# q and k loaded once per batch, their pooled sums taken from PSUM, and layer one's float64 words landing in place

## The chip, the core and the metric

One NeuronCore of a Trainium2 chip runs the whole kernel in one launch. The metric is the device time of that launch in microseconds (us). Three runs of the kernel before took 962.6, 950.5 and 953.72 us, so its median is 953.72. The traces come from a profiled execution, which took 953.08 us.

In the rows, PE is TensorE's matmul stream and PEld its weight loads, DVE is VectorE, ACT is ScalarE, POOL is GpSimd, and SP is SyncE, whose queue issues all the DMAs spoken of here. PSUM is the memory that TensorE writes and that DVE and ACT read.

## The reference

Inputs are q, k, v of [4 batches, 8 heads, 576 tokens, 64] in float32 and two pairs of float64 weights, w_in [512, 2048] and w_out [2048, 512]. The attention has two branches, and their sum goes through two layers:

```
q_d, k_d, v_d = mean of every 4 tokens of q, k, v          # 144 pooled tokens
out_up    = repeat(softmax(q_d k_d^T / 8) v_d, 4 times)    # pooled attention
mask      = |i - j| < 4
out_local = softmax(where(mask, q k^T / 8, -1e9)) v        # band attention
x = (out_up + out_local) as [2304 tokens, 512]
x = relu(x @ w_in1)^2 @ w_out1                             # layer one
y = relu(x @ w_in2)^2 @ w_out2                             # layer two
```

## The kernel before

**Matmuls.** Every fp32 product of the two layers is made of three passes over a high and a low part of both factors (xH, xL and w..0, w..1). The 2304 tokens are 9 tiles of 256, and d_ff is cut into 8 slices p of 256 columns. A step is one slice for one tile: the first product h (L868), then relu and square on ACT and the split into high and low on ACT and DVE (helper `low_g`), then the second product y (L950; in layer two, seven products at L933). Layer one's steps 0 to 15 take tiles 0 and 1 in turns, slice by slice; step 16 is the first of tile 2, step 72 the first of layer two, and there are 144.

**Weights.** The weights arrive as 64-bit words. `convert` takes half of a (slice p, kind) pair, 128x512 words, into one of the landing buffers, and ACT (L698, L700, L373) and DVE (L702, L706, L719) turn them into a high and a low fp32 part. Layer two's pairs are converted too, and written to scratch in DRAM for a later reload. There are four landing buffers ld0 to ld3. Some weight buffers whose words come late serve as further landing buffers, or as buffers of the softmax, until then (the names e..).

**Attention.** Local attention works in groups of 116 queries, five to a batch. Before, `group` loads 128 tokens of q and of k for each (L547, in runs of 256 bytes), transposes them on PE (L556, 8 matmuls), and ACT copies the result out of PSUM (128x1024). Then come the mask (L574), the scores (L583), the softmax on DVE and ACT (L594 to L616), its transposes (L620), and the product with v (L638; v in `values`, 64-KB loads at L532), which with `outd` of the pooled branch gives xr (L650). `split_x` makes xH and xL (L846).

The pooled branch loads q and k a second time in `pool_qk`: six loads of 384 KB per batch (L419), whose runs are 3072 bytes long; two adds per load (L423, L425), on DVE for batches 0 and 1 and on POOL for 2 and 3; three transposes (L431); and two copies by ACT into qd or kd. `pool_v` does as much for v (L403, L407). `heads_of` then makes scores (L454), softmax (L459 to L474), transposes (L481) and the product with the pooled v (L492), and ACT copies it to outd.

**The order.** Each engine's instructions stand in one fixed sequence, written by a planner (class `Order`) from costs in `dve`, `act`, `pool`, `dma` and from due times: every job (a load, a conversion, a head, a group) is a thread in a lane, and constants such as CP, CD (conversions), GP (groups), QP (q and k) and HP (heads) say for which tile it is due. An engine can't pass an instruction that waits. `fill` puts small bf16 matmuls (L1105) into the gaps that the planner sees on PE ahead of the first layer product.

Of the kernel before, what the change touches and what calls it, by code (L numbers as in the profile page):

```python
# [8 lines left out]
F32 = mybir.dt.float32  # L9
# [11 lines left out]
GD = S // 4  # L21
# [14 lines left out]
NLD, NGA, NQK, NVW, NPB, NHD = 4, 2, 2, 2, 2, 2  # L36
AHEAD = 4
LEAD = 2
XO = 'PQVL'
XN = [2, 2, 2, 3]  # L40
# [6 lines left out]
CP, CD, GP, UP = -0.7, 0, -1.92, -0.78  # L47
QP, VP, HP = -0.52, 0.0, 0.05
# [159 lines left out]
def attention_two_mlp_kernel(  # L208
# [19 lines left out]
    mask16 = [sb.tile([128, 64], BF16, name=f"mask{i}") for i in range(3)]  # L228
    nmb_ = [sb.tile([128, 2, H], F32, name=f"nmb{i}") for i in range(NPB + 2 * XN[0])]
    nm_ = [sb.tile([72, 2, 4], F32, name=f"nm{i}") for i in range(NHD)]  # L230
# [4 lines left out]
    ODD = (0, 4)  # L235
    RISE, FALL, JOIN = {1: 0, 2: 48}, {1: 16, 2: 0}, 5
    wt = {}

    def weight(p, kind, low, layer=1):

        if kind == 0:
            if (p, low) not in wt:
                odd = 64 * (low and p in ODD)
                w = sb.tile([128, odd + 1024], F32R, name=f"w{p}0{low}", tag=f"w{p}0{low}")
                wt[p, low] = [w[:, odd + 256 * k - 4 * (odd > 0 and k == 0):][:, 0:256] for k in range(4)]
                wt[p, low, "all"] = w.rearrange("p (k f) -> p k f", k=4) if not odd else None
                if odd:
                    wt[p, low, 0] = w[:, odd - 4:odd + 516].rearrange("p (k f) -> p k f", k=2)[:, :, 0:256]
                else:
                    wt[p, low, 0] = w[:, 0:512].rearrange("p (k f) -> p k f", k=2)  # L250
                wt[p, low, 1] = w[:, odd + 512:odd + 1024].rearrange("p (k f) -> p k f", k=2)
            return wt[p, low]

        if p < JOIN:
            c = FALL[layer] + 2048 * p
            w = joint
        else:
            shift = FALL if p == 6 else RISE
            if p not in wt:
                wt[p] = sb.tile([128, 2048 + max(shift.values())], F32R, name=f"w{p}1", tag=f"w{p}1")  # L260
            c = shift[layer]
            w = wt[p]
        return w[:, c + 1024 * low:c + 1024 * low + 1024].rearrange("p (f e) -> p f e", f=2)

    gSL = sb.tile([128, 512], F32R, name="gSL")
    ga = [sb.tile([128, 512], F32, name=f"ga{i}", tag=f"ga{i}") for i in range(NGA)]
    early = {}
    for p in (7, 6):
        for low in (1, 0):
            early[p, 0, low] = sb.tile([128, 1024], F32, name=f"e{p}0{low}", tag=f"w{p}0{low}")  # L270
    for p in range(6):
        for low in range(2):
            weight(p, 0, low)
    for p in (7, 6, 5):
        w = sb.tile([128, 2048 + max((FALL if p == 6 else RISE).values())], F32, name=f"e{p}1", tag=f"w{p}1")
        for low in range(2):
            early[p, 1, low] = w[:, 1024 * low:1024 * low + 1024]
    joint = sb.tile([128, 2048 * JOIN + 16], F32R, name="w_out")
    g_ = sb.tile([128, 2048 + 48], F32R, name="g")

# [30 lines left out]
    f_at, f_xr, f_ld, f_ga = Slots(3), Slots(NXR), Slots(NLD, NLD), Slots(NGA)  # L311
    f_vw, f_qk, f_pb, f_hd = Slots(NVW, NVW), Slots(NQK, NQK), Slots(NPB, NPB), Slots(NHD)
# [62 lines left out]
    def dma(nbytes, run=4096):  # L375

        return "SP", nbytes / (16e3 * run / (8.0 + run * 0.037))
# [33 lines left out]
    def pool_qk(b, src, dst, c):  # L411

        if b == 1:
            yield o.at("h", 0, 1)
        n = yield from f_ld.take(b == 0)
# [6 lines left out]
        yield own(b, dve(384), pool(384))  # L422
# [3 lines left out]
        if b:  # L426
            yield o.at("scored", b - 1)
# [732 lines left out]
```

## Time and profile before

| | us |
|---|---|
| median of three runs | 953.72 |
| profiled execution | 953.08 |
| span of its trace | 951.30 |
| first layer product (step 0) | 66.18 |
| tile 2's first product (step 16) | 202.06 |
| layer two's first product (step 72) | 564.01 |

The span runs from the first to the last instruction; 1.8 us of the execution lie outside it. Mean granted clock of TensorE is 0.986 of full speed. Over the span PE is busy 95%, DVE 52%, ACT 58%, POOL 17%, and DMAs move 101.0 MB. These shares mix stages that differ, so the rows below are given by stage: the attention ahead of step 0, steps 0 to 15, the rest of layer one, layer two.

### The profile page before, as it was taken

What the parts mean: (1) busy time and instruction counts of PE and PEld (TensorE: products, weight loads), DVE (VectorE), ACT (ScalarE), POOL (GpSimd) and SP (SyncE); (2) the same over time, 40 slices, a digit from 0 to 9 for tenths busy, and PEclk for the clock granted to TensorE, in tenths of its full rate; (3) what the DMA queues carried; (4) which work ended last, traced back from release to release, by engine and by line L of the source; (5) the groups of instructions that cost most, each with busy time, mean ns of one, the idle gap of its engine ahead of it and who ended that gap; (6) DMA issues with size and microseconds to landing.
All of it is one profiled execution on the core that took longest, in us unless ns stands there. A gap on an engine that the chain in (4) does not pass through costs nothing.

```text
span 951.3 us, 21354 instructions
## 1 busy us (share of the span) xinstructions
PE 908.4 (95%) x8792; PEld 867.4 (91%) x8792; DVE 494.7 (52%) x1042; ACT 550.2 (58%) x1109; POOL 160.5 (17%) x158
## 2 busy tenths in 40 slices
PE   8786998989999999999999999999999999999996
PEld 4456997979999999999999999999999999999996
DVE  4789687234454565654321216555554555545464
ACT  3678796445656766665453657645454554545543
POOL 1000001016245200101354454201010110101000
PEclk9999999989999999999999999999999999999999
DMA  9877775127438557676131444011010101100000
GB/s 225 168 185 195 223 195 153 30 79 173 94 111 191 151 174 233 216 233 204 63 101 34 156 156 129 28 45 45 1 45 2 45 1 46 45 1 24 1 23 23
DMA packets 99553, 101.00 MB, mean 106 GB/s; under 512 B 66688, under 2 KB 72320, under 8 KB 99456
## 3 DMA queue, kind: packets, MB, share of 16 engines
q1 hardware_dynamic: 99456, 99.64, 36.9%
q8 instruction: 69, 1.13, 0.5%
q14 instruction: 28, 0.23, 0.1%
HBM read 80.74 MB, written 18.87 MB: 105 GB/s over the span
## 4 chain that ended last, share of the span: by engine, by line
PE 82%; DVE 4%; DMA 4%; ACT 4%; issue 1%; SPq 0%; ACTq 0%; DVEq 0%
PE h L868 37%; PE y L950 17%; PE at L933 13%; PE y L933 5%; DMA ld<-in_v_dram 2%; DMA ld<-in_moe_w_in_dram 1%; PE at L950 1%; PE at L556 1%; PE at L583 1%; PE at L492 1%; PE at L638 1%; PE h L1105 1%; PE at L481 1%; PE at L454 1%; PE at L620 1%
## 5 line engine op out<-in xcount | busy, mean ns | idle before, releaser
L868 PE MATMUL h<-xH,w 128*128 128x256 f32 x2304 | 315.1, 279 | 0.0
L868 PEld LDWEIGHTS h<-xH,w 128*128 128x128 f32 x2304 | 286.3, 189 | 1.4 <-issue 0.6
L879 ACT ACTIVATE h<-h 128x512 f32<-128x512 f32 x144 | 83.9, 583 | 173.8 <-PE h L868 169.3
L868 PE MATMUL h<-xL,w 128*128 128x256 f32 x1152 | 178.6, 277 | 0.0
L917 DVE TENSOR_TENSOR g<-h,g 128x512 fp32r<-128x512 f32 x144 | 98.6, 684 | 133.6 <-ACT g L890 133.5
L868 PEld LDWEIGHTS h<-xL,w 128*128 128x128 f32 x1152 | 152.9, 188 | 0.0
L913 DVE TENSOR_TENSOR S<-h,S 128x128 f32<-128x128 f32 x144 | 42.0, 292 | 160.5 <-ACT g L890 156.4
L950 PE MATMUL y<-g,w_out 128*128 128x256 f32 x960 | 122.0, 282 | 0.0
L950 PEld LDWEIGHTS y<-g,w_out 128*128 128x128 f32 x960 | 115.2, 191 | 0.9 <-issue 0.6
L846 POOL TENSOR_TENSOR xL<-xr,xH 128x512 fp32r<-128x512 f32 x30 | 39.5, 1333 | 353.7 <-ACT xH L373 353.7
L896 ACT CAST SH<-S 128x512 fp32r<-128x512 f32 x72 | 44.8, 622 | 90.7 <-DVE S L913 88.8
L881 ACT ACTIVATE h<-h 128x512 f32<-128x512 f32 x144 | 84.1, 584 | 3.4
L890 ACT CAST g<-h 128x512 fp32r<-128x512 f32 x144 | 84.5, 587 | 2.0 <-DVE S L913 0.7
L950 PE MATMUL y<-g,w 128*128 128x256 f32 x576 | 72.2, 280 | 0.0
L950 PEld LDWEIGHTS y<-g,w 128*128 128x128 f32 x576 | 67.9, 188 | 1.9 <-issue 1.2
L922 DVE TENSOR_TENSOR gSL<-S,SH 128x512 fp32r<-128x512 f32 x72 | 54.3, 754 | 10.2 <-ACT SH L896 1.2
L702 DVE SCALAR_TENSOR_TENSOR ld<-ld 128x512 int32<-128x512 int32 x64 | 44.4, 694 | 27.8 <-ACT ld L700 27.6
L698 ACT ACTIVATE ga<-ld 128x512 f32<-128x512 f32 x64 | 43.2, 674 | 21.3 <-DMA ld<-in_moe_w_in_dram 5.3
L706 DVE SCALAR_TENSOR_TENSOR ga<-ga,ld 128x512 int32<-128x512 int32 x64 | 45.6, 713 | 1.2
L423 POOL TENSOR_TENSOR ld<-ld 128x384 f32<-128x384 f32 x12 | 13.1, 1093 | 186.4 <-DVE hd L474 154.4
L913 DVE TENSOR_TENSOR S<-S,h 128x128 f32<-128x128 f32 x144 | 41.3, 287 | 5.3 <-ACT g L890 0.7
L700 ACT ACTIVATE ld<-ld 128x512 uint32<-128x512 uint32 x64 | 42.8, 668 | 0.1
(265 smaller groups left out, 1368.3 us busy)
## 6 DMA issues: line engine op xcount, KB each, us to landing
ld<-in_moe_w_out_dram SPq DMA_DIRECT2D x32, 512.0 KB, 4.0
ld<-ws SPq DMA_DIRECT2D x24, 512.0 KB, 3.3
ld<-in_moe_w_in_dram SPq DMA_DIRECT2D x32, 256.0 KB, 5.1
ld<-in_moe_w_in_dram SPq DMA_DIRECT2D x16, 512.0 KB, 3.9
ws<-ga SPq DMA_DIRECT2D x32, 256.0 KB, 3.0
ys<-ld SPq DMA_DIRECT2D x9, 512.0 KB, 2.8
xr<-ys SPq DMA_DIRECT2D x9, 512.0 KB, 4.8
vw<-in_v_dram SPq DMA_DIRECT2D x68, 64.0 KB, 2.9
```

Of the source, the lines that this page charges most:

```text
L702: nc.vector.scalar_tensor_tensor(out=w32[:, :, 0], in0=w32[:, :, 1], scalar=-2 ** 31, in1=w32[:, :, 0], op0=ALU.bitwise_and, op1=ALU.bitwi ...
L706: nc.vector.scalar_tensor_tensor(out=gi, in0=gi, scalar=3, in1=w32[:, :, 0], op0=ALU.logical_shift_left, op1=ALU.bitwise_or)
L868: nc.tensor.matmul(out=o, lhsT=w[kk][:, fs], rhs=x[:, kk], start=(i == 0), stop=(i == len(mms) - 1))
L879: nc.scalar.activation(out=h, in_=h, func=AF.Relu)
L881: nc.scalar.activation(out=h, in_=h, func=AF.Square)
L890: nc.scalar.copy(g_of(i, 0), h)
L896: nc.scalar.copy(late2["SH"], late2["S"])
L913: nc.vector.tensor_tensor(out=dst, in0=a, in1=b, op=op)
L917: nc.vector.tensor_tensor(out=g_of(i, 1), in0=h, in1=g_of(i, 0).bitcast(F32), op=ALU.subtract)
L922: nc.vector.tensor_tensor(out=gSL, in0=late2["S"], in1=late2["SH"].bitcast(F32), op=ALU.subtract)
L933: nc.tensor.matmul(out=seven(n, m - 1), lhsT=lhsT, rhs=quarter(p, w, low), start=p == 0 and x == 0 and m not in (2, 3, 6), stop=p == NP - ...
L950: nc.tensor.matmul(out=yb[e // 2][:, (e % 2) * 256:(e % 2) * 256 + 256], lhsT=w[:, fi, e * 128:e * 128 + 128], rhs=g[:, fi * 256:fi * 256 ...
```

## The change: what it does

- `load_qk` takes the place of `pool_qk` and of the loads in `group`. A batch's q and k come once, in five chunks of 128 tokens (the last has 64), in runs of 256 bytes. A chunk is transposed (L431, 8 matmuls), ACT copies it out to `qkT`, and DVE sums every 4 tokens of the same PSUM tile into `qkd` (L438, a `tensor_reduce` over 128x1024). There is one `qkT` for all batches, so a chunk of batch b waits for the local scores of batch b-1 that read it, and for that batch's pooled scores.
- `heads_of` waits for the pooled v and for all local groups of the batch before ahead of its transposes; there is one `outd` instead of two.
- `convert1` loads the words of a whole pair into the buffer that will hold the pair's parts, and converts 1024 wide, or in two halves of 512 (ga0, ga1). Layer two's conversion is `convert2`, as before in halves of 512.
- The landing buffers are ld0, ld1 and gp instead of four; gp is lent to the conversions of layer one until these are done. The buffers lent early change (XO, XN). Conversions are due 0.55 tiles apart (CD), heads 0.15 tiles earlier (HP), and the planner's price of a DMA rises.

```diff
-CP, CD, GP, UP = -0.7, 0, -1.92, -0.78
-QP, VP, HP = -0.52, 0.0, 0.05
+CP, CD, GP, UP = -1.2, 0.55, -2.0, -0.78
+QP, VP, HP = -0.52, 0.0, -0.1
...
-        return "SP", nbytes / (16e3 * run / (8.0 + run * 0.037))
+        return "SP", nbytes / (16e3 * run / (10.0 + run * 0.047))
...
-    def pool_qk(b, src, dst, c):
-
+    def load_qk(b, c):
+
+        n = min(128, S - 128 * c)
         if b == 1:
             yield o.at("h", 0, 1)
-        n = yield from f_ld.take(b == 0)
-        lf = ld[n].bitcast(F32)
-        t = lf[:, 0:768].rearrange("p (g r d) -> p g r d", g=3, r=4)
-        yield dma(128 * 3072, 3072)
-        nc.sync.dma_start(
-            out=lf[:, 0:768], in_=src[b].rearrange("h (p g) d -> (h p) (g d)", p=16)[:, c * 768:(c + 1) * 768]
+        i = yield from f_ld.take(b < 2)
+        raw = ld[i].bitcast(F32)[0:n].rearrange("p (z e) -> p z e", z=2)
+        for z in range(2):
+            tt = yield dma(n * 2048, 256)
+            nc.sync.dma_start(
+                out=raw[:, z].rearrange("p (h d) -> p h d", h=H),
+                in_=(q, k)[z][b, :, 128 * c:128 * c + n].rearrange("h s d -> s h d"),
+            )
+        if b:
+            for g in range(max(0, c - 1), min(NG, c + 2)):
+                yield o.at("lscored", b - 1, g)
+            yield o.at("scored", b - 1)
+        yield lambda: tt
+        a = yield from f_at.take()
+        yield "PE", 0.9
+        for z in range(2):
+            for m in range(4):
+                nc.tensor.transpose(pair[a][:, z, 128 * m:128 * m + n], raw[:, z, 128 * m:128 * m + 128], ident[0:n, 0:n])
+        got = pair[a].rearrange("p z (m s) -> p z m s", m=4)[:, :, :, 0:n]
+        tt = yield act(8 * n)
+        evac(qkT[:, :, :, 128 * c:128 * c + n], got)
+        f_ld.put(i, tt)
+        ev["qkT", b, c] = tt
+        tt = yield dve(8 * n)
+        nc.vector.tensor_reduce(
+            out=qkd[:, :, :, 32 * c:32 * c + n // 4], in_=got.rearrange("p z m (g r) -> p z m g r", r=4),
+            op=ALU.add, axis=AX.X,
         )
...
         yield own(b, dve(576), dve2(576), pool(576))
         engine().tensor_tensor(out=p4, in0=p4, in1=sm.unsqueeze(2).to_broadcast([72, 4, GD]), op=ALU.mult)
+        yield o.at("vpooled", b)
+        if b:
+            yield o.at("local", b - 1)
         a = yield from f_at.take()
...
+        st = early[p, kind] if (p, kind) in early else buffer(p, kind, I64, "s")
+        st = st[:, 0:1024]
...
+        m = yield from f_ga.take()
+        parts = [(gp, 0, 1024)] if m == 0 else [(gb[i], 512 * i, 512) for i in range(2)]
```

**The order at three places.** On SP, the start of the program before: six pooled loads of q and k come first, and the loads of the local groups after them.

```order
L419 DMA ld0_106<-in_q_dram 128x768
L419 DMA ld1_107<-in_k_dram 128x768
L419 DMA ld2_108<-in_q_dram 128x768
L419 DMA ld3_109<-in_k_dram 128x768
L419 DMA e601_81<-in_q_dram 128x768
L419 DMA e600_82<-in_k_dram 128x768
L547 DMA e51_97<-in_q_dram 128x8x64
L547 DMA e51_97<-in_k_dram 128x8x64
```

And now: ten loads of chunks, and then v and the first weights.

```order
L418 DMA ld1_104<-in_q_dram 128x8x64
L418 DMA ld1_104<-in_k_dram 128x8x64
L418 DMA e61_95<-in_q_dram 128x8x64
L418 DMA e61_95<-in_k_dram 128x8x64
L418 DMA e61_95<-in_q_dram 128x8x64
L418 DMA e61_95<-in_k_dram 128x8x64
L418 DMA e60_92<-in_q_dram 64x8x64
L418 DMA e60_92<-in_k_dram 64x8x64
L396 DMA e60_92<-in_v_dram 72x4x256
L396 DMA e51_96<-in_v_dram 72x4x256
L396 DMA ld0_103<-in_v_dram 72x4x256
L659 DMA s00_86<-in_moe_w_in_dram 64x2x256 x2
```

The pooled loads are gone, the local chunks stand in their place, and v and the weights follow.

On PE, the last instructions ahead of tile 2's first product (the last row), before. hd0 and hd1 are the pooled softmax of batch 1, at0 is the one PSUM tile that all of these use:

```order
L481 MATMUL at0_123<-ident_63,hd0_121 72x72 x8
L950 MATMUL at1_124<-g_99,w61_1623 128x256 x8
L950 MATMUL at1_124<-g_99,w71_1796 128x256 x16
L492 MATMUL at0_123<-hd0_121,vd_118 64x144 x4
L950 MATMUL at1_124<-g_99,w71_1796 128x256 x8
L481 MATMUL at0_123<-ident_63,hd1_122 72x72 x8
L492 MATMUL at0_123<-hd1_122,vd_118 64x144 x4
L638 MATMUL at0_123<-pb0_114,vw0_112 64x58 x16
L638 MATMUL at0_123<-pb1_115,vw1_113 64x58 x16
L574 LDWEIGHTS ident16_64
L574 MATMUL at0_123<-mask1_66,ident16_64 128x256
...
L556 MATMUL at0_123<-ident_63,ld3_109 128x128 x8
L868 MATMUL h0_126<-xH0_100,w000_83 128x256
```

And now, around the same product (the row of L858 with x8):

```order
L941 MATMUL at1_116<-g_94,w61_1509 128x256 x16
L431 MATMUL at0_115<-ident_63,ld1_104 128x128 x8
L941 MATMUL at1_116<-g_94,w61_1509 128x256 x8
L941 MATMUL at1_116<-g_94,w71_1716 128x256 x24
L604 MATMUL at0_115<-ident_63,pb0_83 128x128 x4
L858 MATMUL h0_118<-xH0_97,w00_457 128x256 x8
L858 MATMUL h0_118<-xL0_99,w00_457 128x256 x4
L622 MATMUL at0_115<-pb0_83,vw0_106 64x58 x16
```

Batch 1's heads now stand between steps 4 and 11 and the products with v of its first two groups at steps 13 and 14; one transposed chunk, one softmax transpose and the third group's product with v (L622) are left here.

On SP, the queue of the same stretch now. ys is the result of layer one on its way to DRAM, vw are the v rows of a local group:

```order
L418 DMA gp_105<-in_q_dram 128x8x64
L418 DMA gp_105<-in_k_dram 128x8x64
L418 DMA ld0_103<-in_q_dram 128x8x64
L418 DMA ld0_103<-in_k_dram 128x8x64
L537 DMA vw0_106<-in_v_dram 64x4x64 x4
L537 DMA vw1_107<-in_v_dram 64x4x64 x4
L1056 DMA ys0_120<-ld1_104 128x1024
L537 DMA vw0_106<-in_v_dram 64x4x64
L418 DMA ld1_104<-in_q_dram 64x8x64
L418 DMA ld1_104<-in_k_dram 64x8x64
L537 DMA vw0_106<-in_v_dram 64x4x64 x3
```

The third group's v (the last row) now stands behind a load into ld1, and that behind the store of ys0 from ld1.

## Rows read from the trace of the kernel before

**Rows 1.** Windows by stage: stretch, us; busy us (xinstructions) per engine; PEclk, DMA share, GB/s

```profile
0.00:24.00 24.00, 19.81 (x127) 10.44 (x128) 10.01 (x25) 7.51 (x15) 3.03 (x18) 1.00 0.93 224
24.00:66.20 42.20, 34.28 (x452) 21.77 (x450) 34.75 (x77) 29.53 (x73) 0.00 (x0) 0.93 0.76 170
66.20:101.50 35.30, 26.96 (x281) 25.31 (x280) 29.71 (x57) 29.00 (x51) 0.00 (x0) 0.89 0.82 208
101.50:154.60 53.10, 50.12 (x439) 48.94 (x438) 42.16 (x75) 45.41 (x90) 0.00 (x0) 1.00 0.74 202
154.60:202.10 47.50, 38.60 (x405) 35.44 (x403) 18.92 (x38) 20.24 (x52) 7.71 (x8) 0.91 0.19 53
202.10:564.00 361.90, 361.90 (x3838) 351.44 (x3837) 154.46 (x277) 215.80 (x434) 112.38 (x109) 1.00 0.51 150
564.00:951.30 387.30, 376.77 (x3266) 374.05 (x3264) 204.71 (x498) 202.70 (x396) 37.40 (x23) 1.00 0.10 35
```

**Rows 2.** Timeline of PE at two first products: start us, us, instruction xcount

```profile
66.18 1.66 PE L868 MATMUL h<-xH,w 128*128 128x256 f32 x8
202.06 1.95 PE L868 MATMUL h<-xH,w 128*128 128x256 f32 x8
```

**Rows 3.** Windows of two stretches of steps 0 to 15 with low clock

```profile
91.10:97.90 6.80, 5.83 (x29) 5.39 (x28) 5.35 (x11) 5.46 (x11) 0.00 (x0) 0.50 0.61 187
162.80:166.20 3.40, 3.40 (x20) 3.17 (x20) 1.83 (x3) 2.71 (x6) 0.11 (x1) 0.50 0.00 0
```

**Rows 4.** Waits of PE, 66.2 to 202.1: line <- releaser: us, times, longest

```profile
PE at L481 <- ACT hd L464: 4.3, 1, 4.3
PE at L620 <- DVE pb L616: 3.6, 1, 3.6
PE at L620 <- DVE pb L602: 3.0, 1, 3.0
PE at L556 <- DVE pb L602: 1.5, 1, 1.5
```

**Rows 5.** Timeline of DVE ahead of the first layer product

```profile
59.24 0.69 DVE L719 TENSOR_TENSOR w_out<-ga,w_out 128x512 fp32r<-128x512 f32 x1
59.85 0.69 DVE L846 TENSOR_TENSOR xL<-xr,xH 128x512 fp32r<-128x512 f32 x1
```

**Rows 6.** Groups of DVE by form, 0 to 66.2: busy us, mean ns | idle before

```profile
L600 DVE TENSOR_REDUCE nmb<-at 128x8 f32<-128x512 f32 x4 | 2.7, 687 | 5.6 <-PE at L583 5.6
L423 DVE TENSOR_TENSOR ld<-ld 128x384 f32<-128x384 f32 x4 | 2.2, 557 | 1.4 <-DMA ld<-in_q_dram 0.8 <-DMA ld<-in_k_dram 0.5
L425 DVE TENSOR_TENSOR ld<-ld 128x192 f32<-128x192 f32 x4 | 1.4, 358 | 0.1
```

**Rows 7.** Groups of ACT by form, 0 to 202

```profile
L373 ACT ACTIVATE qk<-at 128x1024 f32<-128x1024 f32 x5 | 5.1, 1015 | 1.0 <-PE at L556 1.0
L373 ACT ACTIVATE qd<-at 64x192 f32<-64x192 f32 x12 | 4.4, 364 | 6.7 <-PE at L431 6.6
```

**Rows 8.** Timeline of PE, transposes and fills at the start

```profile
8.75 1.91 PE L1105 MATMUL h<-ident 128*128 128x512 bf16 x4
...
13.47 1.04 PE L556 MATMUL at<-ident,e 128*128 128x128 f32 x8
14.34 0.49 PE L431 MATMUL at<-ident,e 128*64 128x128 f32 x3
...
44.22 2.33 PE L1105 MATMUL h<-ident 128*128 128x512 bf16 x10
```

**Rows 9.** Windows of two stretches of DMA: 256-byte runs, then 3072-byte runs

```profile
228.00:240.00 12.00, 12.00 (x133) 11.06 (x132) 7.07 (x13) 6.27 (x22) 9.04 (x9) 1.00 0.98 196
...
0.00:12.00 12.00, 7.85 (x24) 3.32 (x25) 6.60 (x19) 4.08 (x9) 3.03 (x18) 1.00 0.86 248
```

**Rows 10.** DMA issues: out<-in queue op xcount, KB each, us to landing

```profile
ld<-in_q_dram SPq DMA_DIRECT2D x17, 256.0 KB, 4.6
...
ys<-ld SPq DMA_DIRECT2D x9, 512.0 KB, 2.8
...
vw<-in_v_dram SPq DMA_DIRECT2D x68, 64.0 KB, 2.9
```

More of the change, by code (lines that the diff above doesn't have):

```diff
@@ L227, in attention_two_mlp_kernel @@
     ident16 = sb.tile([128, 128], BF16, name="ident16")
[L228 to L236, printed above, removed]
-    wt = {}
-    def weight(p, kind, low, layer=1):
[L241 to L277, printed above, removed]
@@ L278, in attention_two_mlp_kernel, with columns, buffer, first @@
-    joint = sb.tile([128, 2048 * JOIN + 16], F32R, name="w_out")
+    RISE, FALL = {1: 0, 2: 48}, {1: 16, 2: 0}
+    wt = {}
+    early = {}
+    def columns(p, kind):
+        return 2048 + kind * (48 if p == 5 else 16)
+    def buffer(p, kind, dtype, name):
+        n = columns(p, kind) // (2 if dtype == I64 else 1)
+        return sb.tile([128, n], dtype, name=f"{name}{p}{kind}", tag=f"w{p}{kind}")
+    def first(p, kind):
+        if p > 5 or p == 5 and kind:
+            w = buffer(p, kind, F32, "e")
+            for low in range(2):
+                early[p, kind, low] = w[:, 1024 * low:1024 * low + 1024]
+        else:
+            early[p, kind] = buffer(p, kind, I64, "s")
@@ new lines, in weight @@
+    def weight(p, kind, low, layer=1):
+        if (p, kind) not in wt:
+            wt[p, kind] = buffer(p, kind, F32R, "w")
+        c = 1024 * low + kind * (RISE if p == 5 else FALL)[layer]
+        return wt[p, kind][:, c:c + 1024].rearrange("p (k f) -> p k f", k=4 - 2 * kind)
+    mask16, nmb_, nm_ = [], [], []
+    for i, p in enumerate((0, 1, 2, 3, 4, 7)):
+        first(p, 1)
+        if i < 3:
+            mask16.append(sb.tile([128, 64], BF16, name=f"mask{i}"))
+        for _ in range((1, 1, 1, 3, 0, 0)[i]):
+            nmb_.append(sb.tile([128, 2, H], F32, name=f"nmb{len(nmb_)}"))
+        if i == 4:
+            nm_ = [sb.tile([72, 2, 4], F32, name=f"nm{j}") for j in range(NHD)]
+            sb.tile([128, 32], F32, name="gap")
@@ L279, in attention_two_mlp_kernel @@
+    pb_ = [sb.tile([128, 512], F32, name="pb0", tag="gs")]
+    gb = [sb.tile([128, 512], F32, name=f"ga{i}", tag=f"ga{i}") for i in range(2)]
+    for p in range(NP):
+        first(p, 0)
     g_ = sb.tile([128, 2048 + 48], F32R, name="g")
+    first(6, 1)
+    first(5, 1)
     def g_of(i, low):
@@ L393, in pool_v @@
             yield o.at("h", 0, 1)
-        n = yield from f_ld.take(b == 0)
+        n = yield from f_ld.take(b < 2)
         lf = ld[n].bitcast(F32)[0:72]
@@ L452, in heads_of @@
             for j in range(2):
-                js = slice(64 * j, 64 * j + 64)
+                js, m_ = slice(64 * j, 64 * j + 64), (hp + 2 * j) % 4
                 nc.tensor.matmul(
-                    out=s[:, j, qh], lhsT=qd[js, hp, 72 * qh:72 * qh + 72], rhs=kd[js, hp], start=True, stop=True
+                    out=s[:, j, qh], lhsT=qd[js, m_, 72 * qh:72 * qh + 72], rhs=kd[js, m_], start=True, stop=True
                 )
@@ L868, in mm_h @@
             nc.tensor.matmul(
-                out=o, lhsT=w[kk][:, fs], rhs=x[:, kk], start=(i == 0), stop=(i == len(mms) - 1)
+                out=o, lhsT=w[:, kk, fs], rhs=x[:, kk], start=(i == 0), stop=(i == len(mms) - 1)
             )
@@ L1076, in attention_two_mlp_kernel @@
         t = b * S / TN - 2
-        heads += [(t + QP, pool_qk(b, s_, d_, c)) for c in range(3) for s_, d_ in ((q, qd), (k, kd))]
+        heads += [(t + QP, load_qk(b, c)) for c in range(5)]
         heads += [(t + VP, pool_v(b, kh, j)) for kh in range(2) for j in range(2)]
@@ L1081, in attention_two_mlp_kernel @@
         groups += [((b * S + GQ * i) / TN + GP, group(b, i)) for i in range(NG)]
-    def conversions(layer, t0, dt):
-        return [
-            (t0 + dt * p, convert(layer, p, kind, half)) for p in range(NP) for kind in range(2) for half in range(2)
-        ]
+    first_w = [(CP + CD * p, convert1(p, kind)) for p in range(NP) for kind in range(2)]
+    second_w = [(99, convert2(p, kind, half)) for p in range(NP) for kind in range(2) for half in range(2)]
     o.lane(1, [(-9, act_h())])
```

241 lines of the change are left out of this document (107 added, 134 removed).

## The prediction

> **What bounds the kernel now.** I read the windows by stage first [rows 1]. From 202.1 us on PE is busy all the time (361.9 of 361.9 us, then 376.8 of 387.3), so there only PE work or a new wait can move the time. Ahead of that nothing is full: in the first 66.2 us PE is busy 54.1, much of it with fills, and DVE 34.75 of the 42.2 us after 24; in steps 0 to 15, from 66.18 to 202.06 [rows 2], PE is busy 27.0 + 50.1 + 38.6 = 115.7 us and idle 20.2. I call the four stages A (to 66.2), B (steps 0 to 15, 135.9 us), C (to layer two, 361.9) and D (387.3).
>
> What B loses comes in two kinds. The windows with low clock [rows 3] have a granted clock of 0.50, the 1.2 GHz level; with a like stretch from 196.9 to the end of B they hold about 12.5 us of PE busy time, half of which, 6.3 us, is loss. The rest is the idle time, and the waits of PE name it [rows 4]: softmax links (L481 behind the head's exp, L620 behind a group's DVE) that stand in the PE order before their data are ready. So B is 109.4 us of full-clock work, 6.3 of slow clock, 20.2 of waiting.
>
> In A the last link is DVE: its starts lie 0.61 us apart (59.24, 59.85) right up to the second xL, which is what step 0 and step 1 need [rows 5].
>
> **The change part by part.**
>
> *Pooled loads and adds, removed (24 loads, 48 adds, 72 transposes, 48 copies).* Per batch it takes away 2.36 MB, and for batches 0 and 1 the adds on DVE: twelve per batch, six of 0.56 and six of 0.36 us [rows 6]. In their place stand five `tensor_reduce` per batch, 1024 elements wide out of PSUM. No such row exists. The nearest, 512 wide out of PSUM, takes 0.687; between the adds of 192 and 384 columns lie 0.20 us [rows 6], which is 0.53 for 512 more, so 0.69 + 0.53 = 1.22, an estimate. Bounds: 0.69, as if width were free, and twice that. I take 1.2: DVE 5 x 1.2 = 6 us against 6 x 0.92 = 5.5 before. No gain on DVE, then; POOL is relieved of 24 adds, which nobody in C waits for.
>
> *Conversions.* The same 64-bit words are converted in half as many instructions of twice the width. By that slope each merged pair saves some 0.15 us of an engine; DVE and ACT are not full over B, so I cost it at nothing by itself, and its place in the order (below) is what counts.
>
> *PE work.* Eight transposes take 1.04 us, three pooled ones 0.49 (their tails overlap, so about 0.4 is work), a fill 0.21 at full clock and 0.43 in the first 12.6 us [rows 8]. Counting the order with such durations: real work in A falls from 22.8 to 18.9, but fills rise from 100 to 152, so A's PE sum goes from 44.1 to 51.3. B gains 32 single transposes, 18 others go, and some group work comes earlier: +3.9. In C the same work is missing, with the pooled transposes of batches 2 and 3: -7.8. D's work is the same.
>
> *A.* DVE's list up to the second xL grows from 37.3 to 45.6 us, because the planner puts more conversions ahead of it, now 1024 wide (fourteen at about 1.14). Its first part needs the pooled v. In SP's new order 2.36 MB of q and k and the v end at 4.06 MB: by the 224 GB/s of the first 24 us 18 us, by the 196 of the 256-byte stretch 21 [rows 1, 9], and with issue and landing about 24. The rest of the list is 29.7 us of work at the spacing of [rows 5]; with 3 us of small waits that ends at 57 to 60. PE's own list ends at 51.3 + 6.4 (thirty fills at half clock) + 3 of waits = 60.7. I take 60.7, a gain of **5.5 us**.
>
> *B.* Its waits come from links in the pooled softmax of batch 1, which stood just ahead of step 16, and from groups whose DVE part ran late. In the new order the heads stand between steps 4 and 11, each link with a slice of layer work behind it that covers 2 us or more, and the groups' products with v two steps earlier. ACT is relieved of 48 small copies of 0.36 us; its big copies stay, twenty of 1.0 us [rows 7]. Conversions staggered by 0.55 of a tile leave 28.7 us of DVE work between the second xL and step 3's split, which puts step 3 at about 88 instead of 101.5; that is most of the gain. Then 109.4 + 3.9 = 113.3 of work, and I leave 5.2 us of losses: 1 for a slow clock at the start, 2 for DVE in steps 3 to 12, 2.2 for one slow-clock stretch. B takes 118.5: **-17.4 us**.
>
> *A new wait at step 16.* The third group's v stands on SP behind a load into ld1, that behind ys0's store from ld1, and that behind the copies which wait for the transposes L431 of the chunk in ld1. From that transpose on: evacuation 1.0 [rows 7], copies 1, issue and store 0.3 + 2.8, two chunk issues 0.8, three issues 1.8, landing 2.9 [rows 10], together 10.6. PE reaches the product with v about 5.5 us after that transpose, so it waits 4.5 to 5, and the clock may fall to 1.2 GHz behind it (up to 1.7, as half of a stretch of [rows 3]). C: -7.8 + 5.5 = **-2.3 us**. Bounds: -7.8 where the store is earlier, +1 where ld1's load must land first as well.
>
> *Landing buffers, DMA.* Three buffers instead of four for batches 2 and 3, but the conversions do not use them any more in layer one, and the bytes fall by 10 MB. In C DMA is busy 51%, and ten chunks have 361.9 us. I cost it at nothing; the cover is PE's stream of layer products, and if it goes, a transposing wait comes instead (third rival).
>
> *D.* Its first steps need converted and reloaded weights, as before; 0, with bounds of -2 and +3.
>
> **The sum** is -5.5 - 17.4 - 2.3 = -25.2, against the profiled execution's 953.08: **928 us**. The median, 953.72, is 0.6 higher, which is inside the spread of its runs.
>
> **A page that speaks against part of it.** In the stretch of 256-byte runs the core moved 196 GB/s, with long runs 248 [rows 9]; so the 2.36 MB at the start cost 12.1 us where long runs would cost 9.5, and that is what A has in it. The Trainium skill, DMA: Bandwidth & Descriptors, section Specifications, asks for at least 512 bytes for line rate, below which a read-modify-write is done; it speaks for the first rival, and what the trace shows of it is the 21% between the two rates.
>
> **The rivals.**
>
> 1. *Short runs delay the start.* All ten loads must have landed, been transposed and reduced before the first head can score; before, six loads with long runs stood ahead. If the first stretch moves not 224 but 170 GB/s, the least that a window with a waiting queue shows [rows 1], the 4.06 MB up to v take 24 us instead of 18, and step 1's weights, which stand behind, come later still. A then gains nothing and may lose 2; 953.1 + 2 - 17.4 - 2.3 = **935**. For: the rate of [rows 9]. Against: the local chunks of batch 0 came in the same short runs before, and the total is smaller. 0.17.
> 2. *New waits for old ones.* B's waits move from links to DVE, which is now asked for wide conversions in front of splits: each link of a head or group may stand behind one 1.2 us instruction instead of one of 0.69. In B there are about 18 such links; at 0.5 each 9 us, and the slow clock with them. B gives back 10 of its 17 and A half of its 5.5: **940**, up to 946. For: DVE had 29.7 of 35.3 us and 42.2 of 53.1 in B's first part [rows 1]. 0.20.
> 3. *Slower: the queue's head blocks.* An SP instruction that waits for its buffer holds all behind it. In C, ten chunks of batches 2 and 3 wait for a buffer, for the scores of the batch before, or both, and the transpose in the middle of layer products waits for the chunk. A load of 256 KB lands after 4.6 us [rows 10], and a stop of PE brings the slow clock, 1.7 lost per 3.4 us [rows 3]. Ten chunks at 4.6 + 1.4 are 60 us: 928 + 57 = **985**. It decides from 2.5 us per chunk (no gain left); 4.4 make it slower by 2%. For: `qkT` is single, and the new loads wait for scores and buffer. Against: before, C ran without any idle time while POOL's adds and as many loads stood in the same queue [rows 1]. 0.09.
> 4. *Everything fits*: A ends at 57 by DVE, no wait at step 16, B loses 1: 944 - 17.4 - 4 - 7.8 - 3 = about **912**. 0.06.
>
> The forecast itself keeps 0.48, with a range of its own of 918 to 937.
>
> **How the numbers follow.** What a measurement of this kernel can tell from no change is about 2%, 19 us; faster is below 934.6, slower above 972.8. Faster: nine tenths of the forecast, 0.43, half of rival 1, 0.08, a tenth of rival 2, and rival 4, 0.06: 0.58. Slower: rival 3, 0.09. Within: the remainder, 0.33. The range reaches from 912 (rival 4) to 950 (rival 2 with A's gain gone as well), leaving out rival 3 and a little at each end.
>
> **What would show it.** Right: first product of step 0 near 61, step 3 near 88, step 16 near 61 + 118 = 179, and one wait of 4 to 5 us of L622 for v just behind it; then C near 356 + 4 and D unchanged at 387. The `tensor_reduce` row near 1.2 us. Wrong: a step 0 at 66 or later with DVE or PE waiting for q or k (rival 1); step 16 behind 187 with PE waits on DVE's conversions or reductions (rival 2); PE idle in C with L431 waiting for a chunk (rival 3). A C stage longer than 362 us makes the forecast wrong whatever A and B do.

## The result, and the profile after

The changed kernel took 932.28 us (median of six runs, 927.73 to 942.34) beside 955.77 for the kernel before on the same chips. The ratio is 0.974, 95% interval 0.969 to 0.979: faster. The slowest of the six runs, 942.34, was in a slower state of the chip and is left out of the ratio. The forecast was 928. Its profiled execution took 932.26 us with a span of 930.5, so 1.76 us lie outside, as before.

The windows of the changed kernel, cut at its own first products of step 0, step 3, step 12, step 16 and step 72; columns as in [rows 1]:

```profile
0.00:24.00 24.00, 21.80 (x180) 12.73 (x181) 14.05 (x32) 9.58 (x23) 3.03 (x18) 1.00 1.06 180
24.00:62.82 38.82, 34.79 (x388) 18.90 (x386) 30.50 (x54) 26.82 (x51) 0.00 (x0) 0.96 0.92 207
62.82:91.83 29.01, 26.07 (x249) 24.88 (x249) 24.88 (x41) 22.85 (x33) 0.00 (x0) 0.88 1.06 225
91.83:156.81 64.98, 59.92 (x550) 56.39 (x549) 47.73 (x72) 48.67 (x97) 0.00 (x0) 0.97 0.55 131
156.81:189.41 32.60, 32.60 (x413) 31.27 (x411) 17.65 (x34) 14.23 (x24) 2.53 (x2) 1.00 0.20 50
189.41:543.88 354.47, 354.31 (x3741) 345.37 (x3740) 159.12 (x281) 200.21 (x404) 95.23 (x87) 1.00 0.45 135
543.88:930.50 386.62, 378.09 (x3266) 375.49 (x3264) 205.19 (x499) 202.79 (x397) 36.53 (x22) 1.00 0.11 35
```

By stage this gives, beside the forecast:

| stage | before | forecast change | after | change |
|---|---|---|---|---|
| A, to step 0 | 66.2 | -5.5 | 62.8 | -3.4 |
| B, steps 0 to 15 | 135.9 | -17.4 | 126.6 | -9.3 |
| C, to layer two | 361.9 | -2.3 | 354.5 | -7.4 |
| D, layer two | 387.3 | 0 | 386.6 | -0.7 |
| sum | 951.3 | -25.2 | 930.5 | -20.8 |

The sum came out only 4.4 us short because errors offset each other in part: A and B gave 10.2 us less than forecast, C 5.1 and D 0.7 more. Step 3 came at 91.8 where about 88 was forecast, and step 16 at 189.4 where 179 was forecast; that lies behind 187, which the prediction had named as a sign of its second rival. B is PE busy 118.6 us (115.7 before [rows 1]) and idle 8.0 (20.2 before). What is left of the idle time is in the waits of PE from 62.8 to 189.4:

```profile
PE at L487 <- ACT hd L467: 3.2, 1, 3.2
PE at L604 <- DVE e L600: 1.5, 1, 1.5
PE at L622 <- ACT e L371: 1.0, 1, 1.0
PE at L457 <- ACT hd L467: 0.9, 1, 0.9
PE at L487 <- ACT outd L371: 0.7, 1, 0.7
```

They are of the same kind as in [rows 4], links of a softmax, and shorter. The longest stands in PE's timeline like this:

```profile
108.53 0.71 PE L457 MATMUL at<-qkd 64*72 64x144 f32 x8 [0.87 <-ACT hd L467]
112.41 1.18 PE L487 MATMUL at<-ident,hd 72*72 72x72 f32 x8 [3.16 <-ACT hd L467]
```

The scores of one head (L457) and the transposes of another (L487) are neighbours on PE, with no layer work between them. The transposed head was ready on DVE at 111.34 (L477), but L487 also waited for ACT's exps of the scores just made, which end at 112.36. Both use the PSUM tile `at`.

The place in A where the forecast was late is the last pooled load of v, whose add on DVE starts at 26.81 instead of about 24 (timeline of DVE, with the idle time ahead of it):

```profile
26.81 0.69 DVE L401 TENSOR_TENSOR ld<-ld 72x512 f32<-72x512 f32 x1 [2.09 <-DMA ld<-in_v_dram]
```

The first 24 us moved 180 GB/s, not 224 or 196, and the first weights' words, behind v in SP's queue, were late as well (timeline of ACT):

```profile
28.88 1.12 ACT L674 ACTIVATE gp<-s 128x1024 f32<-128x1024 f32 x1 [5.88 <-DMA s<-in_moe_w_in_dram]
```

Behind that instruction on ACT stands a copy out of PSUM (29.90 to 30.49) for which PE waits, the longest of its waits in A (timeline of PE):

```profile
30.54 0.59 PE L558 MATMUL at<-mask,ident 128*128 128x256 bf16 x2 [4.03 <-ACT pb L371]
```

From there to step 0 at 62.82 PE is busy for 32.27 of 32.28 us, fills among it. So step 0 comes when PE's own list is through, and that list started late because the words did.

And the wait that I had put behind step 16 does not exist. The timelines of SP and of PE there:

```profile
170.02 7.57 SPq L537 DMA_DIRECT2D vw<-in_v_dram  x8
187.50 0.35 SPq L1056 DMA_DIRECT2D ys<-ld  x1
191.58 0.59 SPq L537 DMA_DIRECT2D vw<-in_v_dram  x1
192.26 0.59 SPq L418 DMA_DIRECT2D ld<-in_q_dram  x1
...
193.63 5.02 SPq L537 DMA_DIRECT2D vw<-in_v_dram  x7
```

```profile
189.41 1.17 PE L858 MATMUL h<-xH,w 128*128 128x256 f32 x8
190.41 0.62 PE L858 MATMUL h<-xL,w 128*128 128x256 f32 x4
190.96 0.69 PE L622 MATMUL at<-pb,vw 64*64 64x58 f32 x32
```

PE runs L622 without a wait, since the v of that group are among the eight loads of 170 us, ahead of ys0's store; what stands behind the store belongs to later groups.

### The profile page after: what moved, and what is told of

It is laid out like the page before. It is cut to its first block, busy times and chain, and to the rows that moved or that the text cites. A ratio compares the mean times of both kernels' runs of the same rounds, so it can differ in the third digit from the quotient of the medians.

```text
span 930.5 us, 21004 instructions
## 1 busy us (share of the span) xinstructions
PE 907.6 (98%) x8772; PEld 865.0 (93%) x8772; DVE 499.1 (54%) x1008; ACT 525.2 (56%) x1027; POOL 137.3 (15%) x128
## 4 chain that ended last, share of the span: by engine, by line
PE 88%; DMA 4%; SPq 2%; ACT 2%; DVE 2%; issue 1%; ACTq 0%
PE h L858 40%; PE y L941 19%; PE at L924 13%; PE y L924 5%; PE h L1095 2%; PE at L941 2%; DMA s<-in_moe_w_in_dram 2%; SPq L418 1%; PE at L622 1%; DMA e<-in_v_dram 1%; PE at L431 1%; PE at L567 1%; PE at L497 1%; PE at L487 1%; PE at L604 1%
## 5 line engine op out<-in xcount | busy, mean ns | idle before, releaser
L858 PE MATMUL h<-xH,w 128*128 128x256 f32 x2304 | 317.7, 281 | 0.0
L858 PEld LDWEIGHTS h<-xH,w 128*128 128x128 f32 x2304 | 288.1, 189 | 2.2 <-issue 1.2
L941 PE MATMUL y<-g,w 128*128 128x256 f32 x1536 | 193.7, 281 | 0.2 <-ACT ld L1021 0.2
L941 PEld LDWEIGHTS y<-g,w 128*128 128x128 f32 x1536 | 183.0, 188 | 3.1 <-issue 1.6
L858 PE MATMUL h<-xL,w 128*128 128x256 f32 x1152 | 180.6, 279 | 0.4 <-DVE xL L836 0.4
L858 PEld LDWEIGHTS h<-xL,w 128*128 128x128 f32 x1152 | 154.8, 190 | 0.8 <-DVE xL L836 0.8
L924 PE MATMUL at<-w,SH 128*128 128x256 f32 x224 | 44.6, 281 | 0.6
L1095 PE MATMUL h<-ident 128*128 128x512 bf16 x152 | 38.2, 396 | 1.6 <-DVE ident L1103 1.6
L807 POOL TENSOR_TENSOR w<-ld,w 128x1024 fp32r<-128x1024 f32 x14 | 33.8, 2418 | 38.1 <-ACT w L371 36.0
L924 PEld LDWEIGHTS at<-w,SH 128*128 128x128 f32 x224 | 33.8, 188 | 1.8 <-issue 1.6
L924 PE MATMUL at<-w,g 128*128 128x256 f32 x240 | 34.2, 277 | 0.4 <-DVE g L908 0.4
L924 PE MATMUL at<-w,gSL 128*128 128x256 f32 x112 | 31.7, 283 | 0.7 <-DVE gSL L913 0.4
L924 PEld LDWEIGHTS at<-w,g 128*128 128x128 f32 x240 | 30.4, 188 | 0.6 <-DVE g L908 0.6
```

What stands on the lines that cost most here:

```text
L858: nc.tensor.matmul(out=o, lhsT=w[:, kk, fs], rhs=x[:, kk], start=(i == 0), stop=(i == len(mms) - 1))
L924: nc.tensor.matmul(out=seven(n, m - 1), lhsT=lhsT, rhs=quarter(p, w, low), start=p == 0 and x == 0 and m not in (2, 3, 6), stop=p == NP - ...
L941: nc.tensor.matmul(out=yb[e // 2][:, (e % 2) * 256:(e % 2) * 256 + 256], lhsT=w[:, fi, e * 128:e * 128 + 128], rhs=g[:, fi * 256:fi * 256 ...
L1095: nc.tensor.matmul(out=hb[1], lhsT=ident16, rhs=ident16.unsqueeze(1).to_broadcast([128, 4, 128]), start=True, stop=True)
```

## The experiments

Each kernel's times by stage, from its own trace. D differs between kernels whose layer two is the same, of which the last section tells, so the step-72 column is the better one to compare. The whole times come from several sessions, in which the kernel before took 950.4 (e1 to e4), 954.7 (e5 to e8), 956.0 (e9 to e11) and 953.5 us (e12), beside 955.8 for the changed kernel; across sessions only ratios to the kernel before compare. The table itself says how far a step's time can be trusted. In the changed kernel, e5, e6, e10, e11 and e12, whose edits touch little or nothing ahead of step 0, A lies between 62.6 and 63.9, so differences of about 1 us there say little. C is 354.5 in five kernels and 351.4 in five others with the same work in C, so at step 72 the uncertainty is about 3 us.

| kernel | A | B | C | step 72 at | whole, median |
|---|---|---|---|---|---|
| changed kernel | 62.8 | 126.6 | 354.5 | 543.9 | 932.3 |
| e1 long runs | 57.8 | 124.7 | 354.5 | 536.9 | 928.7 |
| e2 landing only | 71.5 | 118.5 | 367.4 | 557.5 | 953.5 |
| e3 q and k once only | 57.7 | 151.9 | 354.1 | 563.7 | 961.4 |
| e4 constants only | 60.2 | 183.3 | 354.3 | 597.7 | 987.9 |
| e5 half of batch 1 | 63.9 | 126.5 | 351.4 | 541.8 | 930.8 |
| e6 batch 1 twice | 62.6 | 157.3 | 351.4 | 571.3 | 961.0 |
| e7 1-KB runs | 78.1 | 128.3 | 354.5 | 560.9 | 949.4 |
| e8 no fills | 61.6 | 128.7 | 354.5 | 544.8 | 934.3 |
| e9 1-KB runs, spread | 64.4 | 128.2 | 351.4 | 544.1 | 933.5 |
| e10 ACT twice | 63.2 | 133.0 | 351.4 | 547.6 | 937.1 |
| e11 DVE twice | 62.6 | 128.9 | 351.4 | 542.9 | 935.6 |
| e12 high parts on POOL | 63.6 | 127.2 | 354.5 | 545.3 | 935.9 |

**Which part of the change did it: e2, e3, e4.** e2 takes `pool_qk`, `heads_of` and `group` of the kernel before into the changed one:

```diff
-        heads += [(t + QP, load_qk(b, c)) for c in range(5)]
+        heads += [(t + QP, pool_qk(b, s_, d_, c)) for c in range(3) for s_, d_ in ((q, qd), (k, kd))]
```

(One line of the edit.) Its output is not the reference's, for a reason that was not looked for; PE has as many instructions in layer two as before and in the changed kernel (3266).

> The changed kernel with the attention's loads as they were (pool_qk, and q and k again per local group, two outd), so only the words' landing in place, the landing buffers and the constants of the change are left. Theory (C's gain is the pooled transposes, B's is that weights no longer wait for landing buffers): C stays near 362 us as before, B gains a part, but 2.6 MB more per batch stand in a queue that is already full to 117 us; 940 to 950. Rival (loading q and k once is what counts): no gain, 950 to 956. Rival 2 (the landing alone makes it all): 930 to 936.

It took 953.5, ratio to before 1.002 (1.000 to 1.005), which is the range of the first rival and not of the theory. But the stages say more than the verdict. B is 118.5 us, 17.4 less than before, while A is 5.3 longer; the two together end at 190.0, beside 202.1 before and 189.4 in the changed kernel. So landing in place, with the constants and buffers made for it, gives 12.0 of the 12.7 us that the change gains up to step 16. C is 5.5 longer than before: 3.1 are waits of PE, and for as many instructions (3835 and 3838) PE is busy 2.4 us longer. Step 72 is still 6.5 us earlier than before; the profiled execution, the slowest of ten, loses that again in layer two (399.1 us, with 15.6 us of PE idle against 10.5 before and a slower pace).

e3 puts `load_qk` into the kernel before:

```diff
-NLD, NGA, NQK, NVW, NPB, NHD = 4, 2, 2, 2, 2, 2
+NLD, NGA, NVW, NPB, NHD = 3, 2, 2, 2, 2
...
-        heads += [(t + QP, pool_qk(b, s_, d_, c)) for c in range(3) for s_, d_ in ((q, qd), (k, kd))]
+        heads += [(t + QP, load_qk(b, c)) for c in range(5)]
```

> The kernel before with load_qk, tensor_reduce from PSUM and one outd, and with three landing buffers instead of four (the memory for qkT); conversions in halves through the landing buffers and the constants as before. Theory: C loses the 7 to 8 us of pooled transposes; in B the weights still wait for landing buffers, so it gains little or nothing; 943 to 950. Rival (loading once is what counts): 930 to 938.

It took 961.4, ratio 1.012 (1.006 to 1.017), worse than both theories had it. C is 354.1, the 7.8 us that the count of transposes gave, and A is 8.5 shorter; but B is 16.0 longer. Its waits say why:

```profile
PE at L484 <- ACT hd L464: 15.3, 1, 15.3
PE at L454 <- DVE xr L631: 4.6, 1, 4.6
PE at L601 <- DVE e L597: 4.5, 1, 4.5
```

One link of a pooled softmax holds PE for 15.3 us. C's gain is a matter of counts: before, 124 transposes of q and k stand in C, in e3 72 and in the changed kernel 64. Of the 60 that are gone from the changed kernel's C, 36 are the pooled ones of batches 2 and 3, which loading once makes needless; the other 24 are made ahead of C instead.

e4 changes only constants in the kernel before:

```diff
-CP, CD, GP, UP = -0.7, 0, -1.92, -0.78
-QP, VP, HP = -0.52, 0.0, 0.05
+CP, CD, GP, UP = -1.2, 0.55, -2.0, -0.78
+QP, VP, HP = -0.52, 0.0, -0.1
```

(and the price of a DMA, as in the change.)

> The kernel before with only the constants of the change (CP, CD, GP, HP and the planner's price of a DMA). Theory: conversions that are due 0.55 tiles apart while their words pass through four shared landing buffers come later, so B is not shorter, and the whole takes 950 us or more. Rival (the new order of heads and conversions made B's gain, not the loads): 936 to 945.

987.9, ratio 1.039 (1.032 to 1.045): the constants alone cost 4%. Its C is 354.3 although the pooled transposes are still there, and 8.0 of it are waits: about 300 fewer of PE's instructions are left for C (3541 against 3838), since they stand in its long B. So a short C alone says little about loading once. In the whole time none of the three parts is faster than before by itself; by step 72 the landing (e2) is, by 6.5 of the 20.1 us that the change gains there.

**What short runs cost: e1, e7, e9.** e1 keeps order and bytes and leaves out which token belongs on which partition:

```diff
-                out=raw[:, z].rearrange("p (h d) -> p h d", h=H),
-                in_=(q, k)[z][b, :, 128 * c:128 * c + n].rearrange("h s d -> s h d"),
+                out=raw[:, z],
+                in_=(q, k)[z][b].rearrange("h s d -> (h s d)").rearrange("(p e) -> p e", e=512)[128 * c:128 * c + n],
```

> All chunk loads of q and k read runs of 2048 bytes instead of 256, with the same bytes per load and the same order on every engine; what arrives is not the chunk that is asked for, so the output differs. Theory (transport sets the first 117 us of the changed kernel, where the DMA share is 1.0): the 4.7 MB of batches 0 and 1 move at 248 instead of 196 GB/s, 5 us less; step 0 comes 2 to 3 us earlier than 62.8, step 16 about 5 earlier than 189.4, and the whole takes 925 to 928 us. Rival (softmax links, DVE and buffers set B, and short runs are hidden): step 16 within 1 us of 189.4, the whole within 2 us of 932.

Step 0 came 5.05 us earlier, step 16 6.96, and from there to step 72 the distance stays 6.96. More than the theory said in A, and its window shows 230 GB/s up to 12 us where the changed kernel moves 185:

```profile
0.00:12.00 12.00, 10.38 (x57) 6.54 (x58) 4.56 (x10) 4.35 (x4) 3.03 (x18) 1.00 0.86 230
```

SP also issues the ten loads in less time, from 0.74 to 5.69 instead of to 10.55; whether the transfer or the issue is what short runs cost is not told apart by this run. PE's waits in A fall from 6.2 to 3.5 us. In the whole time the gain did not show: the ratio to before is 0.976 (0.972 to 0.981) beside 0.974 for the changed kernel, and layer two took 390.8 instead of 386.6.

e7 tries to have such runs with the right data, for batch 0: a partition holds four tokens of two heads.

```diff
+                for u in range(2):
...
+                    nc.sync.dma_start(
+                        out=raw[:, z, 256 * u:256 * u + 256],
+                        in_=some.rearrange("(g u) (p t) d -> u g p (t d)", u=2, t=4)[u],
+                    )
...
```

> The changed kernel, but batch 0's q and k arrive in runs of 1024 bytes (a partition holds 4 tokens of 2 heads; 16 products with the identity of 64 columns instead of 8 of 128, and two copies and two reductions per chunk instead of one); the result is the reference's. Theory (short runs set A): the first 2.36 MB come 2.6 us sooner, step 0 at 58 to 60 instead of 62.8, and the whole at 926 to 929. Rival 1 (the extra work on PE, ACT and DVE eats it): step 0 at 62 or later, 931 to 936.

Both missed: step 0 at 78.1. In the first 12 us the DMA share is 0.21:

```profile
0.00:12.00 12.00, 7.00 (x42) 4.38 (x44) 1.19 (x7) 2.35 (x3) 3.03 (x18) 1.00 0.21 73
```

The outermost dimension of that load has 4 entries (g). The Trainium skill, DMA: Bandwidth & Descriptors, section "Why a DMA increments its semaphore by 16 and not by 1", says that a load runs on the largest number of engines up to 16 that divides the outermost sizes of both sides. That would be 4 of 16 here, a share of 0.25, and this trace agrees (0.21 over the first 12 us, 0.27 from 6 to 18). e9 puts the 32 groups of tokens outermost (against e7; the copies that read the chunk back follow the new order):

```diff
-                        in_=some.rearrange("(g u) (p t) d -> u g p (t d)", u=2, t=4)[u],
+                        in_=some.rearrange("(g u) (p t) d -> u p g (t d)", u=2, t=4)[u],
```

> As the run with 1024-byte runs for batch 0, but the rows of a load are ordered so that its outermost dimension has 32 entries instead of 4 (there the DMA share was 0.27 and 96 GB/s). Theory (short runs set A, and a load whose outermost dimension is 4 runs on 4 of 16 engines): DMA share near 0.9 and 220 GB/s or more up to 12 us, step 0 at 58 to 60, step 16 at 184 to 187, the whole 925 to 929. Rival (the second copy and reduction per chunk and 16 products of 64 columns eat the gain): step 0 at 62 or later, 931 to 936.

933.5 us, step 0 at 64.4: the rival's time, but the theory's rate did not come about either. The DMA share is 0.56 and the rate 163 GB/s, and SP's timeline shows the twenty loads issued one behind the other, about 0.64 us each:

```profile
3.40 1.25 SPq L423 DMA_DIRECT2D ld<-in_q_dram  x2
4.69 1.25 SPq L423 DMA_DIRECT2D ld<-in_k_dram  x2
5.99 1.25 SPq L423 DMA_DIRECT2D e<-in_q_dram  x2
```

Twenty loads, most of 128 KB, take SP from 0.74 to 13.9 us, longer than the ten with short runs (to 10.55). So e9 does not test longer runs at a higher rate, and what the rival's extra work cost is not told apart from the slow issue. The five us of A that e1 shows were not to be had by splitting loads in this way.

**What holds B: e5, e6, e10, e11, e12.** In the changed kernel DMA is full up to 117 us (share 1.06 in the row of 62.82), and the loads of batch 1 stand ahead of the weights of slices 5 to 7. e5 leaves half of them out:

```diff
+            some = n // 2 if b == 1 else n
+            if some < n:
+                nc.gpsimd.memset(raw[some:n, z], 0.0)
-                out=raw[:, z].rearrange("p (h d) -> p h d", h=H),
+                out=raw[0:some, z].rearrange("p (h d) -> p h d", h=H),
```

> The changed kernel; of batch 1's chunks only the first 64 of 128 tokens are loaded (the other rows are set to zero by POOL, so 1.2 MB of its q and k are left out). Theory (batch 1's 2.36 MB stand on SP ahead of the weights of slices 5 to 7, transport is full to 117 us, ACT waits for the words of a pair and holds the heads' links behind it): 1.2 MB at 230 GB/s is 5 us; the wait of ACT for words at 109 us (5.9 us) and that of PE at L487 (3.2) go or nearly go, step 7 comes 4 to 5 us earlier than 123.5 and step 16 as much before 189.4. Rival (DVE work and the links' own length set it): step 7 within 1 us of 123.5.

The theory fell. Step 7 came at 124.25, 0.8 later (step 0 was already 1.1 later), with DMA share 0.93 instead of 1.07 from 84 to 117 us. It had a misreading in it: the 5.9 us that ACT waits for words end at 28.88, in A, and at 115 ACT waits only 0.8. That short wait is gone here, and PE waits at the same link nearly as long (L490 here is L487 there):

```profile
PE at L490 <- ACT hd L470: 2.7, 1, 2.7
PE at L625 <- ACT e L371: 1.8, 1, 1.8
PE at L607 <- DVE e L603: 1.5, 1, 1.5
```

e6 doubles instead:

```diff
-            nc.sync.dma_start(
+            for _ in range(1 + (b == 1)):
+                nc.sync.dma_start(
...
```

> The changed kernel with each chunk load of batch 1 issued twice, 2.36 MB more. Theory (transport): 10 us at 230 GB/s; step 7 8 to 11 us later than 123.5, step 16 as much later than 189.4, the whole 940 to 943. Rival (buffers or links): only the ten issues of about 0.5 us count, of which nobody waits: step 16 within 3 us.

961.0: step 16 is 30.5 us later, three times what the bytes give, so it says nothing on bytes. A second load into the same buffer waits on SP until the first has landed, and holds all that is behind it:

```profile
76.22 4.05 SPq L419 DMA_DIRECT2D e<-in_k_dram  x2
80.32 4.14 SPq L419 DMA_DIRECT2D e<-in_q_dram  x2
```

That is the third rival's mechanism, at 3 us per load or 6.1 per chunk, where the rival had taken 6.0; in the changed kernel itself it has no such place.

e10 and e11 add work to one engine, for slices 3 to 7, in the same order:

```diff
-            nc.scalar.activation(out=g, in_=wf[:, c:c + n], func=AF.Copy, scale=2.0 ** -112)
+            for _ in range(1 + (p > 2)):
+                nc.scalar.activation(out=g, in_=wf[:, c:c + n], func=AF.Copy, scale=2.0 ** -112)
```

(e10; in e11 the same around DVE's first pass over the words.)

> The changed kernel with ACT's first pass over a pair's words (1.16 us per 1024) done twice for slices 3 to 7, ten pairs, 11.6 us more of ACT between about 45 and 120 us, the same order and result. Theory (B's remaining waits are links of batch 1's pooled softmax that stand behind conversions on ACT): step 0 unchanged, step 7 later than 123.5 by 6 us or more, more than half of what is added. Rival (DVE is the one in front): step 7 later by under 4 us.

> The changed kernel with DVE's first pass over a pair's words (1.22 us) done twice for slices 3 to 7, 12.2 us more of DVE in the same stretch, the same order and result. Theory (ACT is in front): step 7 later than 123.5 by under 5 us. Rival (DVE, busy 27.5 of 31.7 us, is in front): step 7 later by 8 us or more, and the waits of PE at softmax links grow with it.

Step 7 came 6.65 us later for 11.6 us of ACT (0.57 per us) and 1.75 later for 12.2 us of DVE (0.14, little more than the spread), although DVE is the busier of the two. So added work on ACT is nearer to the path. e12 takes ACT's work away:

```diff
+            if p > 2:
+                nc.gpsimd.tensor_copy(hi[:, c:c + n], g)
+            else:
+                evac(hi[:, c:c + n], g)
```

> The changed kernel, but the high parts of slices 3 to 7 (a copy of 1.05 us per 1024 on ACT) are written by POOL, which is idle in B; the same order of everything else, the same result. Theory (ACT is in front in B, 0.57 us of time per us of ACT as the doubled pass showed): 10.5 us less of ACT give 3 to 6 us, step 7 at 118 to 121, the whole at 926 to 929. Rival (a copy on POOL takes some 2.4 us, and DVE's subtraction, which waits for it in order, holds what is behind it): step 7 at 123 or later, 932 to 938.

935.9, ratio to before 0.983 (0.978 to 0.989); step 7 1.4 us later. Between 57 and 125 us ACT is busy 46.58 instead of 53.85, POOL's copy took 1.17 us (not 2.4), and nothing is gained. The link at L487 again holds PE, 3.9 us:

```profile
PE at L487 <- ACT hd L467: 3.9, 1, 3.9
PE at L622 <- ACT e L371: 1.9, 1, 1.9
PE at L604 <- DVE e L600: 1.5, 1, 1.5
```

The traces show why. In the changed kernel the exps ahead of L487 start at 110.83, behind ACT's copies of high parts (109.77 to 110.92), and DVE's part for them (L464) ends at 110.68, behind its conversions: the two engines arrive together. In e12 ACT has no copies there and stands idle 3.11 us until DVE's L464 (112.08). A kernel that relieves both was not run.

**Fills: e8** leaves out the 152 fills.

```diff
-        nc.tensor.matmul(
-            out=hb[1], lhsT=ident16, rhs=ident16.unsqueeze(1).to_broadcast([128, 4, 128]), start=True, stop=True
-        )
+        pass
```

> The changed kernel without the 152 fills, all else in the same order. Theory of the prediction (PE's own list is one of two limits of A, 38 us of its 56.6 busy ones are fills): A ends at DVE's limit, 1 to 3 us earlier, if the clock stays up. Rival (fills hold the clock; without them transposes and links run at 1.2 GHz, and step 0 starts at it): step 0 within 2 us of 62.8, and the first layer steps slower, so step 3 is 3 us or more later.

Step 0 came 1.2 us earlier, step 3 1.7, step 72 0.9 later, the whole at 934.3. The 1.2 us fit both sides and lie within the spread of A; the rival's slower step 3 did not come. But the theory's condition did not hold: from 24 to 61.6 us the granted clock was 0.50, the 1.2 GHz level, instead of 0.96 in the row of 24.00 above, and PE was busy only 22.5 of these 37.6 us. DVE was busy 14.09 of the 14.30 us from 47.7 to 62.0. So two limits lie close together: with fills PE's list sets step 0, without them DVE's list sets it almost as late.

## Why the prediction was right, and where its steps were not

**The total and its sign held**: 932.3 in a range of 912 to 950, in the forecast's own 918 to 937, ratio 0.974. That it came so near is luck in part: B's shortfall of 8.1 us and A's of 2.1 were offset by half, by a wait of 5.5 that had been added to C and does not exist.

**Transposes in C (-7.8)**: right in mechanism and size. C lost 7.4 us, and e3 lost 7.8; in both it is pooled transposes that are gone and other work that stands ahead of C instead, as the prediction had it. The size is uncertain by the 3 us of the pace. The `tensor_reduce` of 1024 columns took 1.22, where 1.2 was taken.

**The new wait at step 16 (+5.5)**: wrong. It rested on a reading of SP's order that gave the loads ahead of ys0's store to the first two groups; the trace has the group's v loaded from 170 us on, ahead of that store. This is what made C 5.1 better.

**A (-5.5)**: right in sign and in the limit that was taken, PE's own list, but 2.1 too large. PE was busy 56.6 us where the forecast had 51.3 + 6.4 = 57.7. (Only six of its first fills took about 0.44 us each, not thirty; the sum still came near.) The term that failed is the "3 of waits": PE waited 6.2 us, 4.0 of them for ACT, which waited for the first weights' words. Behind it is the rate of the first loads: I took 196 to 224 GB/s, and the changed kernel moved 180. The first rival named it, and its mechanism is real: e1 shows that short runs cost 5.05 us of A. A still gained; that this is because fewer bytes stand ahead fits e3, whose A is 8.5 us shorter, but no run has it alone.

**B (-17.4)**: half of it came. The losses that I left in, 5.2 us, are the step that failed: they came to 13.3. Idle time is 8.0, and PE is busy 118.6 where 113.3 of work had been forecast, 5.3 more; the clock rows of 62.82 to 156.81 (0.88 of 29.0 us, 0.97 of 65.0) are some 11 us at the 1.2 GHz level, about 5 of them lost (an estimate: half of the time at that level), which is that much. I had said that every link of batch 1's heads has 2 us or more of layer work behind it. The one at L487 has none: the scores of the next head stand right ahead of it on PE. PE stands 3.2 us there, and 2.7 to 5.0 in e1, e5, e10, e11 and e12, whatever is taken from or added to transport, ACT or DVE. B is 1.9 us shorter with long runs (e1), little more than the spread. e2's B did take the forecast's 118.5, but behind an A that is 8.7 us longer than the changed kernel's, so it does not show that 17.4 was in reach. That the link would go if the planner put it later in PE's sequence was not tried, and stays open.

**The second rival** (old waits replaced by new ones on DVE) came in part. Its sign, step 16 behind 187, came; its 940 did not. The link that stayed waits for ACT and DVE alike: adding to ACT costs four times what adding to DVE does, but with ACT relieved DVE's conversions hold it (e12).

**The third rival** (head of the SP queue) did not come in C, where PE waited 0.2 us in all. e6 shows what it costs once a load waits for another.

**The arithmetic.** Two slips in the recorded sums change nothing: the parts of "faster" add up to 0.59 and not 0.58, and the fourth rival's -3 has no term of its own.

## What to carry to other kernels

When a fixed order is made by a planner, count a link of a softmax by what stands between its two ends on the waiting engine's own list, not by the engines' shares; relief of one busy engine gives nothing when a second one arrives at the link at the same time. Parts of a change that gain nothing in the whole time by themselves can gain together, so a part's price is to be asked with the other part in place, and by stages. When loads are rearranged for longer runs, look at how many engines a load is spread over and at the number of issues before looking at bytes.

## What the runs showed of the hardware that was not expected

Layer two is the same work in every kernel here. Over most of it PE is busy without a break and the granted clock is 1.00, and yet its pace differs. Matmuls started in the same 80 us, first the changed kernel, then e3:

```profile
720.00:800.00 80.00, 79.90 (x703) 79.68 (x703) 43.15 (x108) 41.57 (x83) 5.42 (x4) 1.00 0.08 28
```

```profile
720.00:800.00 80.00, 80.00 (x682) 79.89 (x681) 41.78 (x107) 40.94 (x81) 5.35 (x4) 1.00 0.08 27
```

That is 3%, with no wait in it. The same is seen inside layer one: from 500 to 540 us PE is busy throughout and starts 342 matmuls in the changed kernel, e1 and e7, and 355 in e5, e9 and e10, whose program is the same there; this is where a C of 354.5 or 351.4 comes from. D ran from 385 to 394 us in kernels other than e2, so a gain of 5 us ahead of it can be hidden or doubled in one execution; the step-72 time is the steadier measure. The cause is open.

The reduction and ACT's copy only read the same PSUM tile, and yet the one starts when the other has ended (copy 11.17 to 12.20, reduction at 12.23, with DVE idle 1.16 us ahead of it); ten of the twenty reductions are released by the copy in this way, with 10.1 us of idle DVE ahead of them, some of which goes to the transposes. Each reduction waits for a semaphore of ACT, so the program orders them; whether the chip would let both read at once, no run here shows.
